# Attention with a K and V cache on one core: more P V chunks wait for the next scores, and the last V tile but one becomes a stationary operand as the last is

**Chip, cores, metric.** One core of one Trainium2 chip. The number is device time in microseconds (us). A median is given with its lowest and highest run. The calls of the study ran on different chips, but each had the kernel before on its own chip beside it. So kernels are compared by their ratio to that.

## The reference

One decode step: layer norm of x (4 x 512), attention of one query per head over a cache of 8192 keys (4 sequences, 32 heads, head size 128), and beside it a gated feed-forward block; the three are added.

```
q = (xn @ wq) as 4 x 32 x 1 x 128
p = softmax(q k_cache^T / sqrt(128))      # k_cache, v_cache: 4 x 32 x 8192 x 128, bf16
o = p v_cache
out = x + o @ wo + (silu(xn @ w_gate) * (xn @ w_up)) @ w_down
```

K and V are 268 MB each, and each element is used once. The page of the kernel before shows 550.77 MB moved, by packets that fill 98.8% of the span of 16 DMA engines: reading sets this kernel's time, except where the work on chip leaves the DMA queue without orders.

## The kernel before

The cache is cut into 32 pairs of tiles (K n, V n), 8.39 MB each. A tile holds one sequence and four heads. Three slots of that size take K and V tiles in turn, and a new load is issued when the last reader of its slot is done.

For one pair, VectorE transposes K in 32 pieces and TensorE (PE) makes two score matmuls per piece (`sps`). Softmax follows, then 64 chunks of P V (`oacc`). A matmul here has a stationary operand, whose load the profile shows by itself (PEld: 4884 loads to 4884 matmuls), and one whose columns stream; in a chunk P is stationary and 512 columns of V stream. The last `LO` chunks of V are kept back and run between the score pieces of the next K, so that PE has work while VectorE transposes (PE still waits 163.7 us in all for the transposes). K i+1 takes the slot of V i-2, so its load is issued right behind the last kept chunk.

```python
    def pv_chunk(n, k):                     # 512 columns of V stream, P is stationary
        ...
        mm(o_acc[j % 2][b * QB:b * QB + w, :], pt[n][:, off:off + (w - 1) * QB + 1:QB],
           v_cols(n, k * 512, (k + 1) * 512), start=(k == 0))

    def pv_last(xps, t0, t1, start=False):  # 128 x 128 of V is stationary, 4 columns of P stream
        n = NT - 1
        for t in range(t0, t1):
            ...
            mm(xps[:, :, B - 1], v_cols(n, t * Dh, (t + 1) * Dh), pt[n][...], start=(start and t == t0))

    LO = 12
    for i in range(NT - 1):
        for p in pieces(i, 0, NP):          # 32 pieces: transpose, two score matmuls
            if i >= 3 and p in (6, 10, 14):
                pv_to(i - 2, NK - LO + (p - 2) // 4 * (LO // 3))
                if p == 14:
                    load_k(i + 1)
        ...                                 # load_v(i), softmax, P V of i - 1 up to NK - LO
```

The end, for the last pair (n = 31), is written out by hand. V 31 comes in two halves. The second half waits for a slot that V 30 holds, so it can be issued only behind V 30's last chunk:

```python
    n = NT - 1
    load_wo(t_); v_from(n, t_, H * D, 0, (T // 4, T // 4))     # wo and the first half of V 31
    for p in pieces(n, 0, NP):
        ...
        if p > 8 and p % 3 == 0:
            pv_to(n - 1, (p - 6) * NK // (NP - 8))             # V 30, chunks between the scores
    pv_to(n - 1, NK)
    t_ = slot()
    v_from(n, t_, 0, T // 2, (48, 32, 24, 16, 8))              # second half of V 31, in five parts
    max_1(n); wo_some(2); max_2(n); wo_some(H); pt_turn(n); row_sums(n); fin_1(JL)
    xps = x_tile()
    pv_last(xps, 0, T - TL, start=True)
    fin_2(JL, xps, B - 1)
    pv_last(xps, T - TL, T)
    fin_3(JL, xps)                                             # normalises: writes otn
    wo_some(H)                                                 # last 8 matmuls, then the output
```

Of the kernel before, what the change touches and what calls it, by code (L numbers as in the profile page):

```python
# [15 lines left out]
def kernel(  # L16
# [16 lines left out]
    B, Sq, D = A_x.shape  # L33
    _, H, Sk, Dh = A_k_cache.shape
# [7 lines left out]
    NT = M // HT  # L42
    T = HT * Sk // P
# [30 lines left out]
    def mm(out_ap, lhsT, rhs, start, **kw):  # L74
        nc.tensor.matmul(out_ap, lhsT=lhsT, rhs=rhs, start=start, stop=True,  # L75
                         skip_group_check=True, **kw)

    def slot():
        return slots.tile([P, SLOT], dt.bfloat16, name="slot")
# [11 lines left out]
    def load_k(n):  # L91
        j, b = divmod(n, B)
        t_ = slot()
        nc.sync.dma_start(out=t_[:], in_=A_k_cache[b, j * HT:(j + 1) * HT, :, :].rearrange("h (p t) d -> (h p) (t d)", t=T))
        k_tiles[n] = t_

    def load_v(n, parts=(T,)):
        t_ = slot()
        v_from(n, t_, 0, 0, parts)

    def v_from(n, t_, base, t0, parts):

        j, b = divmod(n, B)
        src = A_v_cache[b, j * HT:(j + 1) * HT, :, :].rearrange("h (p t) d -> (h p) (t d)", t=T)
        v_tiles[n, t0 * Dh] = (t_, base)
        for w in parts:
            nc.sync.dma_start(out=t_[:, base:base + w * Dh], in_=src[:, t0 * Dh:(t0 + w) * Dh])
            base, t0 = base + w * Dh, t0 + w

    def v_cols(n, c0, c1):  # L110
        h0 = max(c for m, c in v_tiles if m == n and c <= c0)
        t_, base = v_tiles[n, h0]
        return t_[:, base + c0 - h0:base + c1 - h0]
# [90 lines left out]
    for half in range(NH):  # L204
        for par in range(2):
            for x in range(8):
                mm(qt_ps[:, half, par, x, :], q_bf[:, half, par, x, :, :], pick,
                   start=(half == 0 and par == 0 and x == 0))
# [6 lines left out]
    def load_ffn():  # L215
        t_ = slot()
        w, w3 = EC * F, 2 * EC * F + FC * D
        nc.sync.dma_start(out=t_[:, 0:w], in_=B_w_gate.rearrange("(p c) f -> p (c f)", c=EC))
        nc.sync.dma_start(out=t_[:, w:2 * w], in_=B_w_up.rearrange("(p c) f -> p (c f)", c=EC))
        nc.sync.dma_start(out=t_[:, 2 * w:w3], in_=B_w_down.rearrange("(p c) e -> p (c e)", c=FC))  # L220
        ffn["w"] = (t_[:, 0:w].rearrange("p (c f) -> p c f", c=EC),
                    t_[:, w:2 * w].rearrange("p (c f) -> p c f", c=EC),
                    t_[:, 2 * w:w3].rearrange("p (c e) -> p c e", c=FC))
# [40 lines left out]
    def build_q(n):  # L264
        j, b = divmod(n, B)
        for a in range(NQ):
            h = j * HT + a
            half, cg, hh = h // 16, (h % 16) // 4, h % 4
            nc.vector.tensor_copy(  # L269
                out=zq[a * QB:(a + 1) * QB, :, XO + a * QB].rearrange("p (j r) -> p r j", r=2),  # L270
                in_=qt[a * QB:(a + 1) * QB, half, :, hh * 2:hh * 2 + 2, cg * B + b])

    def t_piece(n, g, jb):

        w = TG * Dh
        kt = kt_pool.tile([P, w // 2], dt.bfloat16, name="kt")
        src = k_tiles[n][:, g * w:(g + 1) * w].bitcast(dt.uint32).rearrange("p (t j r) -> p t j r", j=2, r=QB)
        nc.vector.transpose(out=kt[:].bitcast(dt.uint32).rearrange("p (t r) -> p t r", r=QB), in_=src[:, :, jb, :])  # L278
        kts[n, g, jb] = kt

    def s_piece(n, g, jb):
        if g == 0 and jb == 0:
            s_ps[n] = psS.tile([P, 512], dt.float32, name="sps")
        kt = kts.pop((n, g, jb))[:].rearrange("p (n r) -> p n r", r=2)
        off = XO - 2 * g
        for r in range(2):
            mm(s_ps[n][:], zq[:, 2 * jb + r, off:off + P], kt[:, :, r], start=(g == 0 and jb == 0 and r == 0))

    def max_1(n):
        mx = small.tile([P, 1], dt.float32, name="mx")  # L290
        nc.vector.reduce_max(out=mx[:], in_=s_ps[n][:], axis=AX.X)  # L291
        nmx[n] = mx
# [18 lines left out]
    def pt_turn(n):  # L311
        p_ = pt[n]
        t_ = ptz
        for y in range(HT):
            nc.vector.transpose(out=t_[y * QB:(y + 1) * QB, :, y, :, :].rearrange("p s u x -> p s (u x)"),  # L315
                                in_=p_[y * QB:(y + 1) * QB, :].rearrange("p (s w) -> p s w", s=4))
        pt[n] = t_[:].rearrange("p s y u x -> p (s y u x)")
# [9 lines left out]
    def p_off(k):  # L327
        g, s = divmod(k, TG // NV)
        return s * HT * NV * QB + 2 * g

    def pv_chunk(n, k):
        j, b = divmod(n, B)
        w = HT * NV
        off = p_off(k)
        mm(o_acc[j % 2][b * QB:b * QB + w, :], pt[n][:, off:off + (w - 1) * QB + 1:QB],
           v_cols(n, k * 512, (k + 1) * 512), start=(k == 0))

    def pv_last(xps, t0, t1, start=False):

        n = NT - 1  # L340
        for t in range(t0, t1):
            k, u = divmod(t, NV)
            off = p_off(k) + u * QB
            mm(xps[:, :, B - 1], v_cols(n, t * Dh, (t + 1) * Dh),
               pt[n][:, off:off + (HT - 1) * NV * QB + 1:NV * QB], start=(start and t == t0))

    def fin_1(j):
        o_sb = kt_pool.tile([P, NV, Dh], dt.float32, name="kt")
        nc.scalar.copy(out=o_sb[:].rearrange("p u d -> p (u d)"), in_=o_acc[j % 2][:])  # L349
        nc.vector.tensor_tensor(out=o_sb[:], in0=o_sb[:], in1=rowu[:].unsqueeze(2).to_broadcast([P, NV, Dh]), op=ALU.mult)  # L350
        o1 = pp.tile([P, Dh], dt.float32, name="o1")
        nc.vector.reduce_sum(out=o1[:], in_=o_sb[:].rearrange("p u d -> p d u"), axis=AX.X)  # L352
        osb[j] = o1

    def x_tile():
        return psX.tile([P, HT, B], dt.float32, name="xps")

    def fin_2(j, xps, nb):
        mm(xps[:, :, 0:nb], osb.pop(j)[:], rowy[:, :, 0:nb], start=False)
# [15 lines left out]
    def wo_mm(i):  # L375
        for half in range(2):
            mm(yo_ps[half][0:B, :], otn[:, i, :], wo_t[0][:, i * D + half * DH:i * D + (half + 1) * DH], start=False)

    NK = T // NV
    NP = 2 * NTG  # L380
    JL = H // HT - 1
    LO = 12
    TL = 80
    wo_next, wo_ready = 0, 0
    pv_at = {n: 0 for n in range(NT)}
# [1 line left out]
    def wo_some(n):  # L387
        nonlocal wo_next
        while n > 0 and wo_next < wo_ready:
            wo_mm(wo_next)  # L390
            wo_next += 1
            n -= 1

    def pv_to(n, k):
        while pv_at[n] < k:
            pv_chunk(n, pv_at[n])
            pv_at[n] += 1

    def pieces(n, p0, p1):
        for p in range(p0, p1):  # L400
            t_piece(n, *divmod(p, 2))
            s_piece(n, *divmod(p, 2))
            yield p - p0 + 1
# [3 lines left out]
    for i in range(NT - 1):  # L407

        for p in pieces(i, 0, NP):
            if i >= 3 and p in (6, 10, 14):  # L410
                pv_to(i - 2, NK - LO + (p - 2) // 4 * (LO // 3))
                if p == 14:
                    load_k(i + 1)
            if p == 16 and i > 0:
                pt_turn(i - 1)

        if i == 0:
            load_ffn()
        elif i == 1:
            load_k(2)  # L420
        elif i == NT - 2:
            load_v(i, (T // 4,) * 4)
        else:
            load_v(i)
        max_1(i)
        build_q(i + 1)

        j, b = divmod(i - 2, B)
        if i > 0:
            pv_to(i - 1, 8)  # L430
        max_2(i)
        if i > 2 and b == B - 1:
            pv_to(i - 1, 16)
            fin_1(j)
            pv_to(i - 1, 36)
            fin_q(j)
            wo_ready = (j + 1) * HT
        if i > 0:
            pv_to(i - 1, NK if i in (1, NT - 2) else NK - LO)
        row_sums(i)  # L440
        if i == 1:
            load_v(1)
            do_ffn()
            load_k(3)

    n = NT - 1
    t_ = slot()
    load_wo(t_)
    v_from(n, t_, H * D, 0, (T // 4, T // 4))
    for p in pieces(n, 0, NP):  # L450
        if p == 6:
            pt_turn(n - 1)
        if p > 8 and p % 3 == 0:
            pv_to(n - 1, (p - 6) * NK // (NP - 8))
    pv_to(n - 1, NK)
    t_ = slot()
    v_from(n, t_, 0, T // 2, (48, 32, 24, 16, 8))
    max_1(n)
    wo_some(2)
    max_2(n)  # L460
    wo_some(H)
    pt_turn(n)
    row_sums(n)
    fin_1(JL)
    xps = x_tile()
    pv_last(xps, 0, T - TL, start=True)
    fin_2(JL, xps, B - 1)
    pv_last(xps, T - TL, T)
    fin_3(JL, xps)
    wo_ready = H  # L470
    wo_some(H)
# [37 lines left out]
```

## Time and profile before

| kernel before | |
|---|---|
| time | 1300.92 us (1298.29 to 1302.07), 3 runs |
| profiled run | span 1299.7 us, granted clock 0.939 |
| K landings, one tile to the next V's | 19.3 us, or about 20.1 us |
| second half of V 31 issued / landed | 1279.56 / 1293.17 us |
| last normalisation (`otn`) begins | 1295.02 us |

A landing is that of the slowest of the 16 DMA engines, and the mean DMA share does not show it: the trace has 16 semaphore updates for the last part of V 31's first half, the first at 1276.19, the median at 1276.61 and the last, its landing, at 1281.81, while the share was down to 0.08 from 1278 to 1280. Most of the lines for these rows stand in the prediction; the last row's is this:

```profile
1295.02 0.18 DVE L362 TENSOR_TENSOR otn<-xps,rcp 128x16 bf16<-128x16 f32 x1 [5.25 <-PE xps L75]
```

VectorE waits here for PE, which by the prediction's lines had hardly paused since 1279.46.

### The profile page before, as it was taken

What the parts mean: (1) busy time and instruction counts of PE and PEld (TensorE: products, weight loads), DVE (VectorE), ACT (ScalarE), POOL (GpSimd) and SP (SyncE); (2) the same over time, 40 slices, a digit from 0 to 9 for tenths busy, and PEclk for the clock granted to TensorE, in tenths of its full rate; (3) what the DMA queues carried; (4) which work ended last, traced back from release to release, by engine and by line L of the source; (5) the groups of instructions that cost most, each with busy time, mean ns of one, the idle gap of its engine ahead of it and who ended that gap; (6) DMA issues with size and microseconds to landing.
All of it is one profiled execution on the core that took longest, in us unless ns stands there. A gap on an engine that the chain in (4) does not pass through costs nothing.

```text
span 1299.7 us, 12521 instructions
## 1 busy us (share of the span) xinstructions
PE 1114.6 (86%) x4884; PEld 443.6 (34%) x4884; DVE 819.1 (63%) x1509; ACT 34.1 (3%) x79; POOL 3.6 (0%) x11
## 2 busy tenths in 40 slices
PE   1898898888898988797988898988887988888889
PEld 0244333333333323333323333323333333333335
DVE  3956656677556576565676655676565776566744
ACT  1000000000000000000000000000000000000000
POOL 1000000000000000000000000000000000000000
PEclk8897999989999999999998989999999989999898
DMA  9999999999999999999999999999999999999996
GB/s 420 420 434 438 428 440 430 436 434 436 426 426 436 430 426 440 426 428 436 426 424 424 423 442 424 424 422 442 424 426 438 420 415 432 424 418 442 422 409 257
DMA packets 12611, 551.57 MB, mean 424 GB/s; under 512 B 1276, under 2 KB 1800, under 8 KB 3080
## 3 DMA queue, kind: packets, MB, share of 16 engines
q1 hardware_dynamic: 12536, 550.77, 98.8%
q8 instruction: 38, 0.62, 0.2%
q14 instruction: 21, 0.17, 0.0%
q10 hardware_dynamic: 16, 0.01, 0.0%
HBM read 550.77 MB, written 0.00 MB: 424 GB/s over the span
## 4 chain that ended last, share of the span: by engine, by line
DMA 57%; PE 37%; DVE 4%; issue 1%; ACT 0%; SPq 0%; DVEq 0%
DMA slot<-in_A_k_cache_dram 57%; PE sps L75 23%; PE oacc L75 12%; DVE kt L278 2%; PE yo_ps L75 1%; DVE ptz L315 1%; PE mps L75 1%; PE xps L75 1%; DVE mx L291 0%; PE mps L297 0%; DVE rcp L325 0%; ACT p__385 L306 0%; DVE zq L269 0%; DVE kt L238 0%; SPq L87 0%
## 5 line engine op out<-in xcount | busy, mean ns | idle before, releaser
L75 PE MATMUL sps<-kt,zq 128*128 128x512 bf16 x2048 | 613.4, 419 | 163.7 <-DVE kt L278 163.7
L278 DVE STREAM_TRANSPOSE kt<-slot 128x512 uint32<-128x512 uint32 x1024 | 635.3, 680 | 106.4 <-DMA slot<-in_A_k_cache_dram 47.7
L75 PE MATMUL oacc<-slot,ptz 128*16 128x512 bf16 x1984 | 460.1, 382 | 0.0
L75 PEld LDWEIGHTS <-zq 128*128 128x128 bf16 x2048 | 204.2, 103 | 553.7 <-issue 415.3
L75 PEld LDWEIGHTS <-ptz 128*16 128x16 bf16 x1984 | 196.3, 106 | 245.3 <-issue 59.2
L325 DVE RECIPROCAL rcp<-mps 128x4 f32<-128x4 f32 x32 | 5.9, 185 | 246.2 <-PE mps L75 246.2
L291 DVE TENSOR_REDUCE mx<-sps 128x1 f32<-128x512 f32 x32 | 22.1, 692 | 24.2 <-PE sps L75 24.2
L300 DVE TENSOR_REDUCE nm<-mps 128x4 f32<-128x64 f32 x32 | 7.2, 225 | 24.0 <-PE mps L297 24.0
L269 DVE COPY zq<-qt 32x4 bf16<-32x4 bf16 x128 | 21.2, 165 | 1.3
L372 DVE TENSOR_TENSOR otn<-xps,rcp 32x16 bf16<-32x16 f32 x28 | 4.8, 170 | 21.4 <-PE xps L75 19.3
L75 PEld LDWEIGHTS <-slot 128*128 128x128 bf16 (+1 forms) x402 | 15.3, 117 | 5.1 <-DVE slot L198 2.7
L75 PEld LDWEIGHTS mps<-rowb,rs 128*128 128x128 f32 x64 | 9.5, 187 | 14.7 <-issue 12.7
L75 PE MATMUL mps<-rowb,rs 128*128 128x4 f32 x64 | 12.3, 263 | 1.7 <-ACT p__385 L306 1.7
L350 DVE TENSOR_TENSOR kt<-kt,rowu 128x512 f32<-128x512 f32 x8 | 5.5, 692 | 10.2 <-ACT kt L349 10.1
L297 PE MATMUL mps<-ident_f,mx 128*128 128x128 f32 x32 | 10.3, 323 | 1.0 <-DVE mx L291 1.0
L75 PEld LDWEIGHTS xps<-rowy,o 128*32 128x32 f32 (+1 forms) x226 | 10.5, 155 | 1.3
L75 PE MATMUL xps<-rowy,o 128*32 128x4 f32 (+1 forms) x226 | 10.3, 203 | 0.0
L297 PEld LDWEIGHTS mps<-ident_f,mx 128*128 128x128 f32 x32 | 4.2, 133 | 14.4 <-DVE zq L269 12.5
L75 PE MATMUL yo_ps<-slot,otn 128*4 128x256 bf16 x64 | 8.3, 290 | 0.3 <-DVE otn L362 0.3
L352 DVE TENSOR_REDUCE o<-kt 128x128 f32<-128x512 f32 x8 | 8.3, 1038 | 0.3
L75 PE MATMUL yo_ps<-slot,kt 128*4 128x256 bf16 x28 | 5.9, 404 | 1.6 <-DVE kt L242 1.6
L75 PE MATMUL sps<-slot,xnt_w 128*32 128x512 bf16 x32 | 3.6, 630 | 4.2 <-DMA slot<-in_A_wq_dram 4.2
(148 smaller groups left out, 186.0 us busy)
## 6 DMA issues: line engine op xcount, KB each, us to landing
slot<-in_A_v_cache_dram SPq DMA_DIRECT2D x6, 2048.0 KB, 27.8
slot<-in_A_wq_dram SPq DMA_DIRECT2D x1, 4096.0 KB
slot<-in_A_wo_dram SPq DMA_DIRECT2D x1, 3584.0 KB, 27.2
slot<-in_B_w_gate_dram SPq DMA_DIRECT2D x1, 1792.0 KB, 23.7
slot<-in_B_w_up_dram SPq DMA_DIRECT2D x1, 1792.0 KB, 27.5
slot<-in_B_w_down_dram SPq DMA_DIRECT2D x1, 1792.0 KB, 31.3
slot<-in_A_v_cache_dram SPq DMA_DIRECT2D x1, 1536.0 KB, 6.5
slot<-in_A_v_cache_dram SPq DMA_DIRECT2D x1, 1024.0 KB, 9.4
```

Of the source, the lines that this page charges most:

```text
L75: nc.tensor.matmul(out_ap, lhsT=lhsT, rhs=rhs, start=start, stop=True, skip_group_check=True, **kw)
L269: nc.vector.tensor_copy(out=zq[a * QB:(a + 1) * QB, :, XO + a * QB].rearrange("p (j r) -> p r j", r=2), in_=qt[a * QB:(a + 1) * QB, half, ...
L278: nc.vector.transpose(out=kt[:].bitcast(dt.uint32).rearrange("p (t r) -> p t r", r=QB), in_=src[:, :, jb, :])
L291: nc.vector.reduce_max(out=mx[:], in_=s_ps[n][:], axis=AX.X)
L297: nc.tensor.matmul(mps[:, 0:P], lhsT=nmx.pop(n)[:, 0:1].to_broadcast([P, P]), rhs=ident_f[:, :], is_transpose=True, start=True, stop=True, ...
L300: nc.vector.tensor_reduce(out=nm[:], in_=by_row(mps[:, 0:P]), axis=AX.X, op=ALU.max, negate=True)
L315: nc.vector.transpose(out=t_[y * QB:(y + 1) * QB, :, y, :, :].rearrange("p s u x -> p s (u x)"), in_=p_[y * QB:(y + 1) * QB, :].rearrange( ...
L325: nc.vector.reciprocal(out=rcp[j][:, :, b], in_=mps[:, P:P + HT])
L350: nc.vector.tensor_tensor(out=o_sb[:], in0=o_sb[:], in1=rowu[:].unsqueeze(2).to_broadcast([P, NV, Dh]), op=ALU.mult)
L352: nc.vector.reduce_sum(out=o1[:], in_=o_sb[:].rearrange("p u d -> p d u"), axis=AX.X)
L372: nc.vector.tensor_tensor(out=otn[q0:q1, j * 4:j * 4 + 4, :], in0=xps[q0:q1], in1=r_[q0:q1, y, :].unsqueeze(1).to_broadcast([QB, 4, B]), o ...
```

## The change

It has two parts. In the loop, twenty chunks instead of twelve are kept for the next scores, in four blocks. In the tail, V 30 is multiplied as V 31 is, with tiles of V as stationary operands in blocks of 32 tiles between the scores. Both then add into one PSUM tile. Because V 30 no longer goes through the slow chunks (eight took 1.91 us in the trace of before), the second half of V 31 can be issued sooner; it takes K 31's slot.

```diff
-    def pv_last(xps, t0, t1, start=False):
-        n = NT - 1
+    def pv_still(n, xps, t0, t1, start=False):
...
-    LO = 12
+    LO = 20
...
-            if i >= 3 and p in (6, 10, 14):
-                pv_to(i - 2, NK - LO + (p - 2) // 4 * (LO // 3))
-                if p == 14:
+            if i >= 3 and p in (4, 7, 10, 13):
+                pv_to(i - 2, NK - LO + (p - 1) // 3 * (LO // 4))
+                if p == 13:
                     load_k(i + 1)
...
+    xps = x_tile()
     for p in pieces(n, 0, NP):
...
-        if p > 8 and p % 3 == 0:
-            pv_to(n - 1, (p - 6) * NK // (NP - 8))
-    pv_to(n - 1, NK)
+        if p > 10 and p % 3 == 0:
+            pv_still(n - 1, xps, (p - 12) // 3 * 32, (p - 9) // 3 * 32, start=(p == 12))
...
-    wo_some(2)
+    pv_still(n - 1, xps, T - 32, T)
...
-    xps = x_tile()
-    pv_last(xps, 0, T - TL, start=True)
-    fin_2(JL, xps, B - 1)
-    pv_last(xps, T - TL, T)
+    pv_still(n, xps, 0, T - TL)
+    fin_2(JL, xps, B - 2)
+    pv_still(n, xps, T - TL, T)
```

More of the change, by code (lines that the diff above doesn't have):

```diff
@@ L343, in pv_last @@
             off = p_off(k) + u * QB
-            mm(xps[:, :, B - 1], v_cols(n, t * Dh, (t + 1) * Dh),
+            mm(xps[:, :, n % B], v_cols(n, t * Dh, (t + 1) * Dh),
                pt[n][:, off:off + (HT - 1) * NV * QB + 1:NV * QB], start=(start and t == t0))
```

## The prediction

> **What bounds the kernel now.** I read the page first, then the queue's own waits, the chain, and the last 50 us in stretches and as a timeline. The page says that the transfers are the bound:
>
> ```profile
> PE 1114.6 (86%) x4884; PEld 443.6 (34%) x4884; DVE 819.1 (63%) x1509; ACT 34.1 (3%) x79; POOL 3.6 (0%) x11
> ...
> q1 hardware_dynamic: 12536, 550.77, 98.8%
> q8 instruction: 38, 0.62, 0.2%
> ...
> HBM read 550.77 MB, written 0.00 MB: 424 GB/s over the span
> ```
>
> One queue moves 550.77 MB and its packets fill 98.8% of 16 engines' span. PE at 86% and VectorE at 63% have room. So the loop over the 32 (K, V) pairs can gain only if the queue runs dry somewhere. It hardly does. The view of the K load's line says so:
>
> ```profile
> DMA to landing us min/median/max: 26.2/27.3/33.3
> ```
>
> A K tile of 8.39 MB takes 19.3 us on the engines (the commonest distance between two landings in the trace), so at 27.3 us from issue to landing it stands some 8 us in the queue behind the V tile before it. V tiles are issued earlier still (about 34 us). The chain names K's transfer for 57% and scores plus P V for 35%, but that is a chain of issues followed back: the K issue that it passes through was 7 to 9 us early.
>
> The end is different. By stretches of 1 us (columns: PE, PEld, DVE, ACT, POOL busy, then TensorE clock, DMA share, GB/s):
>
> ```profile
> 1276.00:1277.00 1.00, 1.00 (x6) 0.40 (x5) 0.18 (x1) 0.00 (x0) 0.00 (x0) 1.00 0.31 131
> 1278.00:1279.00 1.00, 1.00 (x7) 0.48 (x5) 0.13 (x1) 0.00 (x0) 0.00 (x0) 1.00 0.08 33
> 1279.00:1280.00 1.00, 1.00 (x6) 0.32 (x5) 0.00 (x0) 0.00 (x0) 0.00 (x0) 1.00 0.08 33
> 1280.00:1281.00 1.00, 1.00 (x7) 0.28 (x5) 0.42 (x1) 0.00 (x0) 0.00 (x0) 1.00 1.00 205
> 1291.00:1292.00 1.00, 1.00 (x44) 1.00 (x41) 0.00 (x0) 0.00 (x0) 0.00 (x0) 0.50 0.39 143
> ```
>
> From about 1276.5 to 1280.5 the queue is nearly dry: the last half of the last V tile (4.19 MB) is not issued before 1279.56. The timeline shows why, and what follows it:
>
> ```profile
> 1276.16 1.53 PE L75 MATMUL sps<-kt,zq 128*128 128x512 bf16 x6
> 1277.62 1.91 PE L75 MATMUL oacc<-slot,ptz 128*16 128x512 bf16 x8
> 1279.46 1.08 PE L75 MATMUL sps<-kt,zq 128*128 128x512 bf16 x4
> 1279.56 2.34 SPq L107 DMA_DIRECT2D slot<-in_A_v_cache_dram  x5
> 1287.59 4.78 PE L75 MATMUL xps<-ptz,slot 128*128 128x4 bf16 x176
> 1292.65 2.32 PE L75 MATMUL xps<-ptz,slot 128*128 128x4 bf16 x80
> 1295.25 1.87 PE L75 MATMUL yo_ps<-slot,otn 128*4 128x256 bf16 x8 [0.27 <-DVE otn L362]
> ```
>
> The reader is to see a period of 3.30 us for three pieces of scores (six matmuls) and eight P V chunks, PE never idle; the issue comes right behind the last chunk of V tile 30, whose slot it takes. After that PE works without a break from 1279.46 to 1295.02 and the rest is a fixed 4.7 us. In before, then, the tail is PE's.
>
> **But the dry stretch is not dry for all.** A share of 0.08 is one engine of sixteen and a little. The packet records show that one: it trails the other fifteen by 5.6 us, finishes its part of the first half of V tile 31 only at 1281.48, and goes on with the second half at 1281.49 without a pause. The last landing is at 1293.17. Whoever trails loses nothing to the late issue, so closing the hole frees fifteen engines and not that one. This decides the size of the gain.
>
> [...]Here 176 tiles of V as weights took 4.78 us, 27.2 ns each, and 80 at the halved clock 29 ns.[...] a stage with 2.9 us of PE idle at 1248 is followed by 3.4 us at clock 0.5, in which a P V chunk takes 0.43 us, not 0.23; and the clock fell during the 176 weight-heavy tiles.[...] each holds one engine up for about 0.95 us.
>
> **The change part by part.** *LO from 12 to 20, blocks at pieces 4, 7, 10, 13.* Nothing is added; eight chunks of 0.245 us (four take 0.98 in the chain) move from behind the softmax to the next scores: 2.0 us of PE out of one stage, into the other. K's next load is issued after piece 13 in place of 14. From K's landing to that issue PE has 26 matmuls of 0.243 and 20 chunks, 11.2 us, in place of 28 and 12, 9.7 us: the K issue comes about 1.5 us later, out of its 7 to 9 us of lead. V's issue shifts by some 1.2 us, out of 15. The engine that trails is never dry, so this is worth 0 in the loop, at most a few tenths of a us of loss. The last score stage starts about 1.2 us later (at 1245.2 in place of 1243.98), because iteration 30 does all chunks of V 29 anyway.
>
> *V 30 as weights.* 64 chunks of 0.23 us, 14.7 us, become 256 tiles of 27.2 to 29 ns, 7.2 us; 224 of them in seven blocks of 32 (0.93 us) behind pieces 12 to 30. A period falls from 3.30 to 6 x 0.243 + 0.93 = 2.4 us, above VectorE's 1.9. Laid out: pieces 7 to 10 at the halved clock end at 1256.2, piece 12 and its block at 1258.1, six periods at 1272.6. The instruction lists show that the last half of V 31 now takes the slot of K 31, so its issue waits for VectorE's 32nd transposition, about 1272.0, 7.5 us sooner than 1279.56 and before the fifteen engines run dry at 1276. Scores end at 1273.6, the last 32 tiles at 1274.5, the wo matmuls (56 x 0.111) about 1281.0.
>
> *V 31.* PE starts on it at 1281.4 in place of 1287.6. The first 128 tiles end at 1285.2. Now the trailing engine decides: 1281.49 plus its 9.8 us for its share of 4.19 MB gives 1291.3, landing 1291.6, against 1293.17 before, when two instruction blocks were fetched in that stretch. Only the last eight tiles are left then: 1291.9. Before, this point was 1295.02. The sum is -3.1 us; the 4.7 us after it stay. 1300.9 - 3.1 = 1297.8.
>
> **The rivals.** *(A) The hole is worth all that it looks.* If the trailing engine's lag were a chance of this run or is caught up, transfers would end near 1286.5, and PE would end the 256 tiles at 1281.4 + 7 + 0.5 = 1289: -6 us, 1295. For it: fifteen engines are free. Against: the lag is 4.7 us at K 31's landing and 5.6 two tiles later, so it is stable. *(B) The clock takes the gain.* In a block of 32 weight loads few columns stream[...]. If it halves, a period is 6 x 0.427 + 0.93 = 3.5 us, as slow as before. [...]PE reaches V 31 at 1288 and the end is that of before, 1300 to 1301. *(C) More instructions.* 192 more pairs are 384 instructions, one and a half blocks of 256; if they fall on the trailing engine, up to +1.5 us: 1299.3. *(D) K's issue becomes late.* 1.5 us in 28 iterations would show as up to 40 us, 1340, if the lead were used up; with 7 to 9 us of lead I give it 1%.
>
> **Range and chances.** The centre is 1297.8. B and C push up by 1 to 3 us, A down by 3; the three times before lie 3.8 us apart, so the choice of runs alone makes about 1.5 us. 1294.5 to 1300.8 should hold it eight times in ten. 2% is 26 us, more than the whole stage that changes, so faster gets 0.01, slower 0.01, same 0.98.
>
> **What would show each step.** Right: transposition 32 and the SP issue near 1272; no stretch of 1 us with a DMA share under 0.5 before the end; xps groups of 32 at about 0.9 us between groups of six sps; the last landing 1291 to 1292 and `otn` following it within 0.5 us, with PE waiting on the DMA; K's issue to landing near 26 us and landings still 19.3 or 20.3 us apart. Wrong: a granted clock near 0.5 through the last scores (B); last landing under 1288 (A) or above 1293 (C); K's latency down at 20 us with idle engines each iteration (D).

1291.9 - 1295.02 gives -3.1 us, and 1300.9 - 3.1 = 1297.8. Three notes:

- "Each holds one engine up" is said of the page's 38 packets of queue q8, 0.62 MB or 16 KB each; their median was 0.94 us. The page counts 9768 matmuls and weight loads, about 257 to a packet, which gives rival C's blocks of 256.
- The trace shows a clock of 0.5 for 3.41 us from 1252.79, and again from 1290.34 to the end; how much work keeps it at 1.0 was not shown, so B's cost is the author's estimate, from 0.427 us a score matmul at clock 0.5.
- In the sum, 9.8 us for the trailing engine's share of 4.19 MB is an estimate from the 19.3 us of a whole tile; in the changed kernel's trace it took 9.84 (landings at 1282.16 and 1292.00). The 0.3 us from that engine's end to the landing was 0.33 for the half before (1281.48 and 1281.81).

## The result, and the profile after

The changed kernel took 1298.82 us (1298.60 to 1299.64, 4 runs) and the kernel before, on the same chip, 1300.31 us (1298.29 to 1302.07, 4 runs). The ratio is 0.999 with a 95% interval of 0.9973 to 1.0008. That is "same" at 2%. Ratios here and below are the mean time of one kernel's runs over that of the other's of the same rounds, so they are not quite the ratio of the quoted medians. Where I turn a ratio into microseconds, I multiply by 1300.

The page of the changed kernel, the lines that answer to those of before:

```profile
PE 1099.1 (85%) x5010; PEld 441.8 (34%) x5076; DVE 823.0 (63%) x1509; ACT 34.1 (3%) x79; POOL 3.6 (0%) x11
...
q1 hardware_dynamic: 12536, 550.77, 99.0%
q8 instruction: 39, 0.64, 0.2%
q14 instruction: 21, 0.17, 0.0%
```

The reader is to see the same 550.77 MB and one packet of TensorE instructions more. PE's busy time is not to be compared, as 66 of its 5076 matmul records are missing here.

The K load's line, for K issued between 60 and 1250 us:

```profile
DMA to landing us min/median/max: 24.5/26.1/34.2
```

K is issued 1.2 us nearer to its landing than before (median 27.3), as planned. The stretches of 1 us in the tail (columns as in the prediction: PE, PEld, DVE, ACT, POOL busy, clock, DMA share, GB/s; a packet's whole time is counted in the stretch where it starts, so a share can pass 1):

```profile
1276.00:1277.00 1.00, 1.00 (x12) 0.78 (x10) 0.99 (x2) 0.18 (x1) 0.00 (x0) 1.00 1.11 475
1278.00:1279.00 1.00, 1.00 (x11) 0.77 (x10) 0.59 (x1) 0.00 (x0) 0.00 (x0) 1.00 1.04 442
1279.00:1280.00 1.00, 1.00 (x12) 0.78 (x10) 0.00 (x0) 0.00 (x0) 0.00 (x0) 1.00 1.01 430
...
1288.00:1289.00 1.00, 0.66 (x24) 0.66 (x25) 0.00 (x0) 0.00 (x0) 0.00 (x0) 0.50 0.37 145
1289.00:1290.00 1.00, 0.36 (x14) 0.27 (x11) 0.00 (x0) 0.00 (x0) 0.00 (x0) 0.50 0.13 53
...
1291.00:1292.00 1.00, 0.58 (x16) 0.51 (x16) 0.00 (x0) 0.00 (x0) 0.00 (x0) 0.50 0.04 16
```

The hole is gone: the share was 0.08 at 1278 and is 1.04. But the same low share appears at the end. By the packet records fourteen engines are done by about 1289.1, a fifteenth at 1291.0, and the last goes on to 1291.7. The timeline shows who waits for it:

```profile
1269.81 1.51 PE L75 MATMUL sps<-kt,zq 128*128 128x512 bf16 x6
...
1271.16 0.98 PE L75 MATMUL xps<-ptz,slot 128*128 128x4 bf16 x32
1271.79 2.23 SPq L107 DMA_DIRECT2D slot<-in_A_v_cache_dram  x5
...
1280.54 3.52 PE L75 MATMUL xps<-ptz,slot 128*128 128x4 bf16 x128
...
1285.87 1.44 PE L75 MATMUL xps<-ptz,slot 128*128 128x4 bf16 x48 [1.80 <-DMA slot<-in_A_v_cache_dram]
...
1291.42 1.01 PE L75 MATMUL xps<-ptz,slot 128*128 128x4 bf16 x24 [0.44 <-DMA slot<-in_A_v_cache_dram]
...
1292.46 0.17 DVE L361 TENSOR_TENSOR otn<-xps,rcp 128x16 bf16<-128x16 f32 x1 [9.74 <-PE xps L75]
```

The issue moved from 1279.56 to 1271.79, 7.8 us. PE reaches V 31 at 1280.54 instead of 1287.59, 7.1 us. The last normalisation moved from 1295.02 to 1292.46, only 2.6 us: PE now waits before each part, and the last landing (1292.00, before 1293.17) sets the end. The chain that ended last says the same in its last link, the fourth of the five parts of that half, which landed at 1291.37:

```profile
1273.11 18.26 DMA slot<-in_A_v_cache_dram
```

The tail changed hands, from PE to one DMA engine.

### The profile page after: what moved, and what is told of

It is laid out like the page before. It is cut to its first block, busy times and chain, and to the rows that moved or that the text cites. A ratio compares the mean times of both kernels' runs of the same rounds, so it can differ in the third digit from the quotient of the medians.

```text
span 1297.1 us, 12866 instructions
## 1 busy us (share of the span) xinstructions
PE 1099.1 (85%) x5010; PEld 441.8 (34%) x5076; DVE 823.0 (63%) x1509; ACT 34.1 (3%) x79; POOL 3.6 (0%) x11
## 3 DMA queue, kind: packets, MB, share of 16 engines
q1 hardware_dynamic: 12536, 550.77, 99.0%
HBM read 550.77 MB, written 0.00 MB: 425 GB/s over the span
## 4 chain that ended last, share of the span: by engine, by line
DMA 59%; PE 35%; DVE 4%; issue 2%; SPq 0%; ACT 0%; DVEq 0%
DMA slot<-in_A_k_cache_dram 57%; PE sps L75 19%; PE oacc L75 14%; DVE kt L278 4%; DMA slot<-in_A_v_cache_dram 1%; PE mps L75 1%; DVE ptz L315 1%; PE yo_ps L75 1%; PE xps L75 1%; SPq L107 0%; ACT p__385 L306 0%; PE mps L297 0%; DVE rcp L325 0%; DVE mx L291 0%; DVE zq L269 0%
## 5 line engine op out<-in xcount | busy, mean ns | idle before, releaser
L75 PE MATMUL sps<-kt,zq 128*128 128x512 bf16 x1982 | 597.2, 421 | 172.9 <-DVE kt L278 172.3
L75 PEld LDWEIGHTS <-ptz 128*16 128x16 bf16 x1920 | 188.9, 107 | 250.1 <-issue 78.0
L75 PEld LDWEIGHTS <-slot 128*128 128x128 bf16 (+1 forms) x658 | 23.3, 110 | 11.6 <-DMA slot<-in_A_v_cache_dram 4.0
L269 DVE COPY zq<-qt 32x4 bf16<-32x4 bf16 x128 | 21.2, 166 | 1.3
L75 PE MATMUL xps<-ptz,slot 128*128 128x4 bf16 x512 | 15.6, 169 | 3.7 <-DMA slot<-in_A_v_cache_dram 3.7
L371 DVE TENSOR_TENSOR otn<-xps,rcp 32x16 bf16<-32x16 f32 x28 | 4.8, 170 | 21.4 <-PE xps L75 19.3
## 6 DMA issues: line engine op xcount, KB each, us to landing
slot<-in_B_w_gate_dram SPq DMA_DIRECT2D x1, 1792.0 KB, 23.9
```

Of the source, the lines that this page charges most:

```text
L75: nc.tensor.matmul(out_ap, lhsT=lhsT, rhs=rhs, start=start, stop=True, skip_group_check=True, **kw)
L269: nc.vector.tensor_copy(out=zq[a * QB:(a + 1) * QB, :, XO + a * QB].rearrange("p (j r) -> p r j", r=2), in_=qt[a * QB:(a + 1) * QB, half, ...
L371: nc.vector.tensor_tensor(out=otn[q0:q1, j * 4:j * 4 + 4, :], in0=xps[q0:q1], in1=r_[q0:q1, y, :].unsqueeze(1).to_broadcast([QB, 4, B]), o ...
```

## The experiments

Three questions were open. Does the tail or the loop bring the gain? Is it the closed hole, or PE being done earlier? And why does one engine trail? All twelve kernels were correct on the chip.

### The change again, and each part alone

The changed kernel itself, for comparison on the same chip. Label r_after.

> The changed kernel again, on the same chip as the three runs beside it, to be compared with them. Theory (the end of the kernel gained about 4 us, the loop gained nothing, and runs differ by about 1 us): 1 to 4 us under the kernel before. Rival (the change is worth nothing beyond the scatter): within 0.7 us of the kernel before.

The tail alone: the changed kernel with the loop of before.

```diff
-    LO = 20
+    LO = 12
-            if i >= 3 and p in (4, 7, 10, 13):
-                pv_to(i - 2, NK - LO + (p - 1) // 3 * (LO // 4))
-                if p == 13:
+            if i >= 3 and p in (6, 10, 14):
+                pv_to(i - 2, NK - LO + (p - 2) // 4 * (LO // 3))
+                if p == 14:
```

> The end of the change alone: V 30 as weights, twelve chunks in three blocks as before. Theory (all of the gain is in the end, none in the loop): the same as the whole change within 0.7 us, so 1 to 4 us under the kernel before; last landing near 1291 to 1293 and DMA share over 0.8 in every us until 1286. The last score stage starts about 1.2 us sooner than with twenty chunks. Rival (the twenty chunks in four blocks bring the gain, or part of it): within 0.7 us of the kernel before.

The blocks alone: the kernel before with `LO = 20` and pieces 4, 7, 10, 13 (the opposite edit, on the kernel before).

> The loop of the change alone: twenty chunks in four blocks, the old end. Theory (K's issue only moves about 1.2 us nearer to its landing, and the DMA engine that ends last is never dry): within 0.7 us of the kernel before; K's issue to landing 26 in place of 27.3 us; the dry stretch of about 4 us before the last load is there, later by about 1.2 us. Rival 1 (the blocks bring the gain): 1 to 4 us under the kernel before. Rival 2 (the later K issue costs its 1.2 to 1.5 us per tile): 30 us or more above.

| kernel (5 rounds; before 1300.65 us, 9 runs) | median us | ratio to before, 95% | K issue to landing, median | `otn` begins |
|---|---|---|---|---|
| changed kernel (r_after) | 1298.45 (1297.93 to 1299.48) | 0.9984 [0.9970, 0.9997] | 25.9 | 1292.00 |
| tail alone (e1_tail) | 1298.28 (1297.22 to 1300.13) | 0.9981 [0.9968, 0.9993] | 27.3 | 1291.93 |
| blocks alone (e2_blocks) | 1302.21 (1301.65 to 1303.35) | 1.0013 [1.0000, 1.0025] | 26.2 | 1295.52 |

The tail alone brings 2.5 us (0.0019 x 1300), all of the gain. The blocks add nothing to it (0.0003 x 1300 = 0.4 us the other way, far within the intervals). Alone, with the old tail, they seem to cost 1.7 us, at the edge of the interval, where under 0.7 was expected. The trace shows 0.5 us of that: `otn` at 1295.52, against 1295.02, as the last score stage began at 1244.99 instead of 1243.98 and PE still set that end. Adding the tail to the blocks takes 0.0029 x 1300 = 3.8 us off; adding it to the kernel before, 2.5.

In the new tail PE waits for the DMA anyway, so a score stage that starts a little later is hidden. In the tail-alone kernel that wait is longer:

```profile
1281.68 1.87 PE L75 MATMUL xps<-ptz,slot 128*128 128x4 bf16 x64 [2.84 <-DMA slot<-in_A_v_cache_dram]
...
1285.34 1.44 PE L75 MATMUL xps<-ptz,slot 128*128 128x4 bf16 x48 [1.80 <-DMA slot<-in_A_v_cache_dram]
```

It waits 2.84 us for the last part of the first half of V 31. In the changed kernel this wait was 0.76 us in one trace (r_after) and absent in the other. Both end where the same transfer does.

### Is it the hole?

The changed kernel with the hole put back: a one-element copy on ScalarE, which reads a result of the `wo` matmuls, writes into the slot before the second half of V 31 is issued.

```diff
-    t_ = slot()
-    v_from(n, t_, 0, T // 2, (48, 32, 24, 16, 8))
     max_1(n)
-    pv_still(n - 1, xps, T - 32, T)
     max_2(n)
+    wo_some(26)
+    t_ = slot()
+    nc.scalar.copy(out=t_[0:B, 0:1], in_=yo_ps[1][0:B, 0:1])
+    pv_still(n - 1, xps, T - 32, T)
+    v_from(n, t_, 0, T // 2, (48, 32, 24, 16, 8))
```

> The changed kernel with the dry stretch put back on purpose: the last half of V 31 is issued near 1279.5 in place of 1271.8, held back by a small copy that reads the output sums after 26 of 28 heads. Results stay right. Theory (one DMA engine trails the others by 4 to 5 us and still works on the first half until 1281, so the late issue starves only the other fifteen): within 0.7 us of the changed kernel, with a DMA share near 0.1 from 1277.5 to 1280.5 and the last landing near 1292. Rival (the filled hole of 3.5 to 4 us is the gain): 3 to 4 us above the changed kernel, at or above the kernel before, last landing near 1295.

It took 1299.47 us (1298.23 to 1300.23), ratio 0.9989 [0.9976, 1.0001], so 0.7 us more than the changed kernel of the same call, and the two intervals overlap. The issue was at 1279.69, as late as before. The edit also moved V 30's last 32 tiles behind most of the `wo` matmuls, and VectorE's transposes of P waited for them (6.15 us), so PE reached V 31 at 1283.37, 2.8 us later than in the changed kernel and 4.2 sooner than before. The stretches show that a hole was there, but a smaller one than before's:

```profile
1277.00:1278.00 1.00, 1.00 (x12) 0.78 (x10) 0.00 (x0) 0.00 (x0) 0.00 (x0) 1.00 1.15 492
1278.00:1279.00 1.00, 1.00 (x12) 0.78 (x10) 0.00 (x0) 0.00 (x0) 0.00 (x0) 1.00 0.50 213
1279.00:1280.00 1.00, 1.00 (x28) 0.75 (x27) 0.00 (x0) 0.48 (x2) 0.00 (x0) 1.00 0.35 147
```

The queue ran low for some 2 us here, from 1278; before's hole lasted from 1276.5 to 1280.5. The last landing came at 1293.32, later than the 1292 expected and sooner than the rival's 1295; `otn` followed at 1293.78. The profiled run was the slowest of its five, and K 31 landed late in it too: from there to the last landing took 49.5 us, against 48.9 in both traces of the changed kernel. So issuing 7.9 us later, with PE early, cost about 0.7 us by the clock and 0.6 in the traces; the scatter of five runs each allows up to about 2. It does not show what a hole of four us would cost. The traces speak for PE reaching V 31 sooner as the source of the gain, and not for the fuller queue. The timing alone does not settle it, as this run's interval includes 1, and a kernel with the hole closed and PE late was not tried.

### Why one engine trails

The records do not number the engines. But while the queue is full a packet starts within 0.01 us of the end of its engine's last one, so they can be strung together. They show that the trailing engine also carries most of the queue q14 of the page, VectorE's instructions: packets of 8 KB, 128 instructions each (0.17 MB in 21 packets). VectorE has 2468 instructions in the changed kernel, semaphores included, so about 19 blocks. The two other packets (at 709.6 and 726.5 us) fell on engines that did not trail. A VectorE packet takes 0.31 us itself, and the data packet behind each took 2.94 to 3.03 us instead of 2.42. I sorted the distances between the last engine's ends of successive 8.39 MB tiles by whether such a packet fell in between (r_after):

| | distance between ends, us | tiles |
|---|---|---|
| no VectorE packet | 19.36 | 41 |
| a VectorE packet | 20.18 | 18 |

The two kinds of landing distance that the prediction speaks of, 19.3 and 20.3, answer to these two rows. TensorE's packets (q8, 16 KB, a median of 0.93 us each in the changed kernel's first trace) make no difference to the distance: 19.37 without and 19.35 with, where q14 had none. That is a correlation, so two runs raised one cost at a time. The first adds 32 tiny instructions per pair on VectorE, eight blocks more. The second adds 32 tiny matmuls with their weight loads per pair on PE, eight blocks of 256 more, twice the bytes (its zeroed tile `xnt_z` is cut from the edit shown).

```diff
         nc.vector.reduce_sum(out=nb[:], in_=nm[:], axis=AX.X)
+        for _ in range(32):
+            nc.vector.memset(pad_t[:, 0:1], 0.0)
```

> The changed kernel with 32 tiny memsets on VectorE per (K, V) pair, right after the softmax, where VectorE idles for some 6 to 12 us: 1024 more instructions, 8 more blocks of 8 KB fetched over DMA. Theory (every block of VectorE's instructions stops one DMA engine, always the same, for about 0.8 us, and that engine sets the pace): 27 packets of 8 KB in place of 19, the interval of two landings 20.1 us where such a fetch falls in and 19.35 elsewhere, and 8 x 0.8 = 6.4 us (5 to 8) above the changed kernel. Rival (the memsets fall into idle time and fetches are hidden): within 1 us of it.

```diff
         nc.vector.reciprocal(out=rcp[j][:, :, b], in_=mps[:, P:P + HT])
+        for _ in range(32):
+            mm(mps[:, 256:260], xnt_z[:], xnt_z[:, 0:4], start=True)
```

> The control: 32 tiny matmuls with their weight loads on PE per pair, behind the row sums where PE waits for the next K tile: 2048 more instructions, 8 more blocks of 16 KB, twice the bytes of the VectorE run. Theory (PE's blocks are fetched by other DMA engines, which wait for the trailing one anyway): within 1 us of the changed kernel. Rival (any instruction fetch takes its time from the transfers): 8 x 0.95 = 7 to 8 us above.

The third has the query copies on ScalarE instead of VectorE (`nc.scalar.copy` for `nc.vector.tensor_copy` in `build_q`), which takes 128 instructions off VectorE.

> The changed kernel with the four small query copies per pair on ScalarE instead of VectorE: 128 fewer VectorE instructions, one block. Theory: one packet of 8 KB fewer, about 0.8 us under the changed kernel (0 to 2, hardly clear of noise). Rival[...]: 0 to 2 us above.

(The rival's reason is cut, as no trace here shows it.)

| kernel (3 rounds; before 1299.69 us, 7 runs) | median us | ratio, 95% | packets q14, q8 |
|---|---|---|---|
| 32 more on VectorE (e4_dve32) | 1306.32 (1305.48 to 1307.53) | 1.0048 [1.0032, 1.0065] | 29, 39 |
| 32 more pairs on PE (e5_pe32) | 1300.34 (1298.51 to 1301.02) | 0.9998 [0.9983, 1.0013] | 21, 47 |
| query copies on ScalarE (e7_qact) | 1298.00 (1297.08 to 1300.77) | 0.9986 [0.9971, 1.0001] | 21, 39 |

The pages of the first two, the queue lines of VectorE's run:

```profile
q1 hardware_dynamic: 12536, 550.77, 98.7%
q8 instruction: 39, 0.64, 0.2%
q14 instruction: 29, 0.24, 0.0%
```

and of PE's:

```profile
q8 instruction: 47, 0.77, 0.2%
q14 instruction: 21, 0.17, 0.0%
```

Against the changed kernel's 0.9984, eight VectorE blocks cost 0.0064 x 1300 = 8.3 us. Eight PE blocks cost 0.0014 x 1300 = 1.8 us. That is more than the 1 us expected, and about what two intervals of 0.0015 allow as chance. In the traces, K 31 lands at 1249.12 with more on VectorE, 1244.47 with more on PE and 1242.62 without. The memsets also occupy VectorE for a while in each pair. On average K's issue did not suffer: it stands 6.1 us ahead of the trailing engine, 6.3 without them. One early K tile did, with 1.6 us of lead: it took 21.1 us, and 1.8 us of the sum is that. The rest fits the fetches: tiles with a VectorE packet took 20.1 us, as in the changed kernel (20.2), and there are eight such packets more. The third run says nothing about time: VectorE has exactly 128 instructions fewer (2340), but the packets stayed 21. The trace points to why. ScalarE went from 120 instructions to 280, and q14 carries its blocks too: one fell at 293.5 us, just after ScalarE's 64th instruction (289), and another at 883.0, after its 192nd (878); r_after has its odd packet at 726.5, after the 64th (721). So VectorE lost one block and ScalarE gained one. The ratio did not move by what the intervals can tell (0.9986 and 0.9984).

### Fewer VectorE instructions

If each fetch costs, fewer should gain. One transpose of 128 x 1024 replaces two of 128 x 512, through two buffers of twice the size. For room, the queries stay in PSUM and a few small tiles share memory (cut here).

```diff
-    kt_pool = ctx.enter_context(tc.tile_pool(name="ktp", bufs=3))
+    kt_pool = ctx.enter_context(tc.tile_pool(name="ktp", bufs=2))
...
-        kt = kt_pool.tile([P, w // 2], dt.bfloat16, name="kt")
-        src = k_tiles[n][:, g * w:(g + 1) * w].bitcast(dt.uint32).rearrange("p (t j r) -> p t j r", j=2, r=QB)
-        nc.vector.transpose(out=kt[:].bitcast(dt.uint32).rearrange("p (t r) -> p t r", r=QB), in_=src[:, :, jb, :])
+        if jb == 0:
+            kt = kt_pool.tile([P, w], dt.bfloat16, name="kt")
+            src = k_tiles[n][:, g * w:(g + 1) * w].bitcast(dt.uint32)
+            nc.vector.transpose(out=kt[:].bitcast(dt.uint32).rearrange("p (t r) -> p t r", r=QB),
+                                in_=src.rearrange("p (t r) -> p t r", r=QB))
```

Applied to the changed kernel:

> The changed kernel with one VectorE transpose of 128x1024 for each two pieces of a chunk, in place of two of 128x512, through two buffers of twice the size; to make room, the queries stay in PSUM and a few small tiles share memory. The program listing has 816 VectorE rows instead of 1330, and with the semaphores beside them about 7 to 9 fewer blocks of 128 instructions to fetch. Theory (each fetch of such a block costs the trailing DMA engine, and with it the kernel, some 0.8 us): the fetching queue shows about 12 packets instead of 21, and the time falls by 6 to 7 us against the changed kernel, to 1291 to 1293 us (0.992 to 0.994 of the kernel before). Rival (the fetches only happen to coincide with the longer intervals): the time stays within 1.5 us of the changed kernel, 1297 to 1300. Third way: the coarser double buffer makes TensorE wait in the score stages, K's issue slips, and the time rises.

Applied to the tail alone (`LO = 12`, three blocks):

> The same paired transposes in the kernel with the new tail alone (twelve chunks kept for the next scores, three blocks). Theory: within 0.7 us of the run before it in this list, since blocks bring nothing; 1291 to 1293 us. If the twenty kept chunks help once VectorE has fewer instructions, this run is slower than that one by over 1 us.

And, since fewer kept chunks looked better, with six (`LO = 6`, three blocks of two):

> The opposite of the change's first part: paired transposes and the new tail, with six chunks kept for the next scores (three blocks of two) instead of twelve. In the traces so far K's issue stands, on average, 7.4 us ahead of the trailing DMA engine's end of the tile before it in the kernel before (twelve chunks), 6.3 in the changed kernel (twenty), 4.2 with twenty-eight, and 5.6 with paired transposes and twelve; where it stood under some 4 us, single tiles took 0.5 to 1.6 us longer. Theory (the reserve of K's issue is what the kept chunks cost): six chunks fewer give about 1.2 us of reserve back, 6.5 to 7 us on average, K tiles longer than 19.6 us without a VectorE fetch go from three to none or one, and the time falls by 0.5 to 1.5 us against twelve chunks, to 1292 to 1293.5 us. Rival (the later release of V's slots costs as much as K's reserve gains, or twelve chunks cost nothing): the same as twelve chunks or slower, 1293.5 to 1296.

### More kept chunks

The changed kernel, and then the blocks with the old tail, with `LO = 28` in place of 20 (seven chunks per block).

> The changed kernel with twenty-eight chunks kept for the next scores instead of twenty. Theory (TensorE is done ahead of the trailing DMA engine, so a later last score stage is hidden): within 0.7 us of the changed kernel, 1298 to 1299.5 us, with the median time from K's issue to its landing near 25 us. Rival (a later issue of K costs the loop): over 1.5 us slower, above 1300.

> The old tail with twenty-eight chunks kept (the kernel with the blocks alone had twenty, and was 1.7 us slower than the kernel before). Theory (with the old tail TensorE sets the end, and the last score stage starts later by about 1 us for each eight chunks more): 2.5 to 3.5 us slower than the kernel before, 1302.5 to 1304 us, and the last normalisation of the outputs 2 to 3 us later than before's 1295.0. Rival (the 1.7 us was noise): within 1 us of the kernel before.

| kernel (5 rounds) | median us | ratio, 95% | q14 | K's lead, mean and least, us |
|---|---|---|---|---|
| paired, LO 20 (e8_pair) | 1296.47 (1293.75 to 1297.82) | 0.9969 [0.9958, 0.9981] | 14 | 5.6, 3.1 |
| paired, LO 12 (e9_pair_tail) | 1293.42 (1293.03 to 1297.24) | 0.9959 [0.9947, 0.9971] | 13 | 5.6, 2.8 |
| paired, LO 6 (e12_pair_lo6) | 1293.71 (1293.04 to 1294.19) | 0.9949 [0.9936, 0.9963] | 13 | 5.8, 3.0 |
| changed, LO 28 (e10_lo28) | 1302.80 (1299.87 to 1307.31) | 1.0025 [1.0009, 1.0041] | 21 | 4.2, 2.8 |
| old tail, LO 28 (e11_lo28_old) | 1308.75 (1304.47 to 1314.52) | 1.0072 [1.0052, 1.0092] | 21 | 4.4, 2.4 |

The kernel before had 1300.07 us in the call of all but e12_pair_lo6, and 1300.28 in that one's. K's lead is the time from K's issue to the trailing engine's end of the tile before it: 7.4 us on average in the kernel before, 6.3 in the changed kernel (r_after), with least values of 4.4 and 4.9.

**Fewer fetches gain, but less than expected.** With twenty kept chunks the gain over the changed kernel was 0.0015 x 1300 = 2.0 us, where 6 to 7 were expected. The packets fell as reckoned: VectorE's instructions went from 2468 to 1448 with twelve kept chunks, which is eight blocks, and q14 from 21 to 13. The page's line of the paired kernel with twelve:

```profile
PE 1068.7 (83%) x5076; PEld 448.5 (35%) x5076; DVE 796.2 (62%) x996; ACT 34.1 (3%) x79; POOL 3.6 (0%) x11
...
q14 instruction: 13, 0.11, 0.0%
```

In the traces its tail transfer ends at 1285.65 instead of 1291.47 with the tail alone, 5.8 us sooner; but the profiled run was the fastest of its five. The ratios give 0.0022 x 1300 = 2.9 us (0.9981 to 0.9959), and those with six chunks 4.2. Twelve chunks were expected within 0.7 us of twenty; they were 1.3 us faster by the ratios, whose intervals overlap. Part of the rest shows in the records of the paired kernel with twenty, whose profiled run was the slowest of its five: seven tiles without a fetch took 19.9 to 21.2 us instead of 19.36. With fewer fetches the trailing engine trails less (the paired kernel with twelve, 13 packets: by the packet records some 2 us behind the median engine on average, against 4.0 in the kernel before with 21), K's lead over it shrinks to 5.6 us, and some tiles then come late. Why some V tiles, whose lead is above 8 us, were also long, is open. Whether six chunks beat twelve is also open: the lead hardly grew (5.6 to 5.8, where 6.5 to 7 was expected), and the intervals overlap.

**More kept chunks cost the loop.** I expected twenty-eight to be hidden in the new tail, and that was wrong: 0.0041 x 1300 = 5.3 us slower than twenty. The K load's line for it:

```profile
DMA to landing us min/median/max: 22.8/24.5/33.0
```

The median is only 1.4 us below twenty's 25.9, but ten tiles without a fetch took 19.6 to 20.9 us, and eight of these are K tiles whose lead was 2.8 to 4.0 us. Nine K tiles without a fetch had a lead of 4.0 us or less, so eight of nine were long; of the nine with more, none was. So in this trace K's reserve runs out near 4 us of lead, not near zero. With the old tail it took 9.4 us (0.0072 x 1300) more than the kernel before, where 2.5 to 3.5 were expected. Its trace has `otn` at 1298.76, 3.2 us after twenty's. That profiled run was one of the faster of six that lie 10 us apart, so the rest of the loss can't be read from it, and it stays open.

The best kernels, the paired transposes with the new tail and six or twelve kept chunks, beat both kernels: 0.9949 and 0.9959 of the kernel before, while the changed one stood at 0.9984.

## Why the prediction was right

The verdict and the range hold: 1297.8 was predicted, 1298.82 and 1298.45 were measured. The range alone tests little, as a kernel without any gain (1300.3) would have fallen into it. The change was foretold at -3.1 us and measured by ratio at -1.3 and -2.1, where the first interval includes no change. The level came out nearer than that because the three runs of before had a median 0.6 us above that of the four, which is luck. It is the steps in the trace that test the mechanism.

- **The tail was PE's, and becomes the trailing engine's: right.** PE starts V 31 at 1280.54 (1281.4 foretold) and waits for the DMA before each part. The last landing is at 1292.00 (1291.6) and `otn` at 1292.46 (1291.9). The sum, -3.1 us, is between the two readings of the tail's part by ratio, -2.5 and -3.8.
- **V 30 as stationary tiles: right, and a little cheaper.** A block of 32 took 0.98 us (0.93), a period of three score pieces and one block 2.19 us (2.4). VectorE's three transposes at 1.90 us nearly fill it: it waits 0.29 us for PE in each period. The issue came at 1271.79 (1272.0).
- **Closing the hole frees fifteen engines and not the one that trails: right in its result.** Fourteen end by 1289.1, one at 1291.0, and the time follows the sixteenth; putting much of the hole back cost 0.7 us, within the noise. The size of a full hole stays untested. Two readings behind it were loose. The lag of 5.6 us is that against most engines, as the next slowest ended that half at 1278.92, 2.6 us ahead. And in before the engine that had trailed went on from 1281.49 level with the others. Another, which a TensorE block stopped at 1285.38, ended its second part last, at 1288.94, and so most likely landed last; the second block, at 1291.39, fell on an engine that had finished. PE set that end, so neither changes the sum.
- **"0 in the loop, at most a few tenths of a us of loss": right for twenty chunks in the new tail (0.4 us), but its reason was too generous.** With the old tail they seem to cost 1.7 us. The prediction counted 7 to 9 us of lead as all free. At twenty-eight chunks a mean lead of 4.2 us already cost 5.3 us. The prediction's step from twelve to twenty happened to stay on the safe side.
- **Rival A (-6 us) fell:** the engine does trail to the end. **Rival B fell:** the halved clock ended at 1258.81, having lasted 6.83 us where the kernel before and r_after had 3.41; then the clock was 1.0 through the later blocks of stationary tiles, up to about 1282.7 (23.9 us). **Rival D** did not happen at twenty chunks; twenty-eight show it beginning.
- **Rival C named the wrong instructions.** It charged TensorE's blocks; the runs that add blocks to one queue at a time show VectorE's: eight of its blocks cost 8.3 us, eight of TensorE's 1.8 us, within the noise. The prediction also took the trail for a stable lag of 5.6 us. In r_after the last engine was 1.5 us behind the median at 104 us and 3 to 5 us behind from 500 us on, growing by some 0.8 us at most VectorE fetches.
- **The shortfall of 0.7 to 1.0 us in the time (1.0 to 1.8 in the change)** has a visible part: the last landing came 0.4 us later than foretold, and PE then had 0.46 us left instead of 0.3. The loop's 0.4 us is as large. None of these is outside the spread of the runs.

## What to carry to other kernels

The slowest of the sixteen engines set the end, and the mean share did not show it: with the hole closed (share 0.08 to 1.04 at 1278) the issue came 7.8 us sooner, but the last normalisation only 2.6, right behind that engine's landing. So in a kernel that its transfers bind, look at that engine first. Measure how much lead each load has over it before spending the lead on a nicer overlap: here it was used up near 4 us, well before it reached zero (LO 28: 5.3 us slower than 20). And count instructions on the off-path engines as well: here most of VectorE's fetches fell on one DMA engine that also carried data, and eight more of them cost 8.3 us.
